# Nyström attention, routing and gated units on one core: ranks in one pass, a table loaded first, and a new order of work

## The chip, the cores and the metric

The kernel runs on one core of a Trainium2 chip. The metric is the time of one execution on the device in microseconds (us), and less is better. Three timed runs of the kernel before gave 581.68, 582.09 and 582.16 us.

## What is computed

Four batches of 576 tokens with 8 heads of 64 go through Nyström attention with 32 landmarks a head. The 2304 rows of 512 that come out are routed to one of 8 experts each, and the result passes through a gated layer of 1536 columns. The core of the reference:

```
q_lm, k_lm = means of 18 tokens each          # 32 landmarks a head
A = softmax(q k_lm'), Bm = softmax(q_lm k_lm'), C = softmax(q_lm k')
Z = Bm' / (norm1(Bm) * norminf(Bm) + 1e-6)
for _ in range(6): Z = 2 * Z - Z @ Bm @ Z
x = A @ Z @ C @ v                              # 2304 rows of 512
logits = x @ w_gate; expert_idx = argmax(logits); gate_w = max of softmax(logits)
for i in range(N):                             # rank of a token in its expert, in order
    if counts[e] < capacity: disp[e, counts[e]] = x[i]; counts[e] += 1
y = relu(disp @ w1) @ w2;  out[i] = gate_w[i] * y[expert_idx[i], pos[i]]
result = (sigmoid(out @ w_gate2) * (out @ w_val)) @ w_out
```

## The kernel before

**Tiling.** TensorE multiplies with 128 partitions of contraction. A product of good accuracy is made in three passes (`PASSES`, L22) over a number split into a high part (`hi`, rounded to the fast format) and the rest (`lo`). Attention of a batch is never multiplied out to rows: its left factor (`at`, the weights A turned and scaled with the gates) stays apart from the right one (`cv`), and the right one is multiplied into an expert's first matrix (`fold`, tile `fold_now`). So an expert's first product over a batch is `mm<-xa` or `mm<-xb`, on tiles of 128x288.

**Blocks.** A batch whose tokens sit with one expert is one block. "lead" is the block of batch 0, for the expert of its token 0; the next one is that of batch 1; the others come from a list that the kernel makes of the counts (`block_list`). After each block's expert (1024 inner columns, product tile `slot`) comes a unit: the gated layer on the same 576 rows, in twelve steps `f`, whose output collects in five accumulators `acc0` to `acc4`; the last four steps are held back and multiplied at the end, accumulator by accumulator (`unit_out`, `HELD`, `ENDS`), and each finished accumulator is copied to `o_tile` and sent off by an indirect DMA of POOL. With this input there are three expert blocks of 576 rows and three units of 768.

**What sets the order.** Each piece of work is a generator (a stream) that yields an engine and the events and buffers that it needs, and then issues instructions. `Streams.go` (L99 to L280) keeps a model of the time of each engine and always takes the stream with the smallest start in the model plus `SLACK` (0.003 us) times its urgency (`URGENCY`, L26). A large number lets others go ahead by 0.3 us per hundred. `SPARED` sets how much earlier DVE must be than ACT to get a copy that either can make. Where TensorE would have little to do, `fill_up` puts in products of no use on the tile `idle`. The order is made when the program is built and then stands; the engines run it in their own order and wait for each other by semaphores. Every operation recorded this way has line L94 in the profile.

**Streams of a batch,** in the order of the data: `load_qk` and `load_v` (SP's queue; at most eight such DMAs are open, since each uses one of eight semaphores in turn, and the DMA that comes back to a semaphore waits for the one that had it), `sums` (landmarks `ld` by DVE), `scores` (products `pa` of q with `ld`, `pb` of the landmarks; the tile `pa` is turned into `ea` by DVE), `inverse` (softmax of `pb` by ACT into `eb`, by DVE into `bb`; norms by `pn`, then `py`, `pz`), `weights` (softmax of `ea`: DVE `ma`, subtraction and sums, ACT exponential, POOL the product with `ra`), `context` (`pc`, ACT `ec`, `pct`, `pv`), `back` (the fold with the router, `pf`, `pw`, `pgt`, `pg`, whose result are the logits; then DVE makes maximum `mx`, difference `dl`, place `mn`, and `lead`, the number of the expert that SP's queue reads to load its matrices `w_raw`), `ranks`, and `gate`, `rows`, `scaled` (DVE spreads the gates as `spread`, PE makes `pgb` of it, DVE scales `at`, ACT casts the high part and DVE subtracts it for the low part of `xa`).

**Ranks before.** `ranks(b)` runs once per batch and waits for the table of the batch before. It makes a one-hot of `mn` in a scan tile of 96x48, its sum `rsum`, two products `pr` (ranks within the batch and the counts of those before), three shifted additions, the rank `r`, the mask of `cap_f`, a tile `spots` and six products `ptb` that write the list of rows by expert (`table_i`). For the lead batches a product `pe` places the lead's own row.

**Start.** Identity, masks and iotas are made on POOL and DVE; `capacity` is loaded by POOL's queue (L394) and cast on DVE (L396). ACT loads the table of its exponential when the first one comes. DVE adds the landmarks of batch 0 as the loads land.

Of the kernel before, what the change touches and what calls it, by code (L numbers as in the profile page):

```python
# [26 lines left out]
    load=60,  # L27
    sums=150,
    inverse=5,
    scores=-100,  # L30
    context=-20,
    back=10,
    weights=60,
    ranks=4,
    lead_rows=0,
    rows=5,
    lead_loads=10,
    lead_split=-20,
    fold=-20,
    lead=20,  # L40
    narrow=40,
)
STEP = 2
SUMS = ()
LOWS = "pool"
SLACK = 0.003
# [52 lines left out]
class Streams:  # L99
# [7 lines left out]
    SPARED = 1.5  # L107
# [176 lines left out]
def tile_attention_moe_glu(  # L284
# [60 lines left out]
    nc.gpsimd.memset(ones, 1.0)  # L345
    iota_c = once.tile([128, P], F32, name="iota_c")
# [13 lines left out]
    spots = once.tile([P, J, E, TC], F32R, name="spots")  # L360
# [153 lines left out]
    def urgency(stage, b):  # L514
        if b == B - 1 and stage in ("inverse", "context", "back", "ranks"):
            return 0
        return URGENCY[stage] + (STEP * b if b in range(B) else 0)

# [187 lines left out]
    def unit_out(b, idx):  # L706
# [12 lines left out]
        for c in ENDS:  # L719
            for f in range(KG - HELD, KG):  # L720
                yield "pe+", *needs(f, c)
                out_rows(b, c, f)
            run.spawn(store_out(c, idx, scatters), run.urgency)
# [67 lines left out]
    with actx:  # L791
# [7 lines left out]
        scans = []  # L799
        for i in range(3):  # L800
            t = ap.tile([P, 4 + J, E], F32, name=f"scan{i}")
            nc.gpsimd.memset(t, 0.0)
            scans.append(t)
        gates = ap.tile([P, B, J], F32, name="gates")
        counts = ap.tile([P, B + 1, E], F32, name="counts")
        nc.gpsimd.memset(counts[:, 0], 0.0)
        wrs = [ap.tile([128, G, LM], F32, name=f"wr{i}") for i in range(2)]
        for t in wrs:
# [5 lines left out]
            nc, dict(bank=7, raw=3, cv=2, qk=6, ea=2, ec=2, xs=1, w=4, ws0=1, ws1=1, ws2=1, ws3=1)  # L814
# [50 lines left out]
        def sums(b, w, g, src):  # L865
            ld = lds[b % 2]
            free = [f"{what}{b - 2}" for what in ("scores", "context", "inverse")]
            for kk in range(2):
                dv = src[:, kk].rearrange("p (c m r) -> p m c r", c=J, r=SEGP)
                dst = ld[:, w, 2 * g + kk]  # L870
                if (b, w) not in SUMS:
                    yield "dve", f"raw{b}{w}{g}{kk}", *free
                    dve.tensor_reduce(dst, dv, AX.XY, ALU.add)
                else:
                    yield "pool", f"raw{b}{w}{g}{kk}", *free
                    s3 = wk.tile([128, J, LM], F32, tag="s3", name=f"s3{w}{b}{g}{kk}", bufs=1)
                    dc = src[:, kk].rearrange("p (c m r) -> p c m r", c=J, r=SEGP)
                    pool.tensor_tensor(s3, dc[..., 0], dc[..., 1], ALU.add)
                    pool.tensor_tensor(s3, s3, dc[..., 2], ALU.add)
                    pool.tensor_tensor(s3[:, 0:3], s3[:, 0:3], s3[:, 3:6], ALU.add)  # L880
                    pool.tensor_tensor(dst, s3[:, 0], s3[:, 1], ALU.add)
                    pool.tensor_tensor(dst, dst, s3[:, 2], ALU.add)
            run.done(f"landmarks{b}{w}{g}")
# [77 lines left out]

        def scores(b):

            ld = lds[b % 2]
            for u in range(2):
# [15 lines left out]
                if u == 1 and b >= 2:  # L981
                    run.release("qk", "qk")
# [8 lines left out]
        def weights(b, u, ea):  # L991
# [6 lines left out]
            yield ("dve",)  # L998
            dve.tensor_tensor(ef, ef, ma.unsqueeze(2).broadcast_to(shape), ALU.subtract)
# [9 lines left out]
            yield ("pool",)  # L1009
            pool.tensor_tensor(ef, ef, ra.unsqueeze(2).broadcast_to(shape), ALU.mult)  # L1010
# [42 lines left out]
        def context_parts(b):  # L1053
# [15 lines left out]
            if b >= 2:  # L1069
                run.release("qk", "qk")  # L1070
# [32 lines left out]
        def back(b):  # L1103
# [64 lines left out]
            mn = wk.tile([P, J], F32, tag="mn", name=f"mn{b}")  # L1168
            yield ("dve",)
            dve.tensor_reduce(mn, eq, AX.X, ALU.min)  # L1170
            if b < LEADS:
# [3 lines left out]
                dve.tensor_scalar_add(lead[:, b, 0:1], mn[0:1, 0:1], 1000.0)  # L1175
# [4 lines left out]
            run.spawn(ranks(b, mn), urgency("ranks", b))  # L1180

        def ranks(b, mn):
            je = [P, J, E]

            def small(tag, shape, dt=F32):
                return wk.tile(shape, dt, tag=tag, name=f"{tag}{b}", bufs=1)

            yield "dve", f"table{b - 1}"
            oh = scans[0][:, 4 : 4 + J]
            dve.tensor_tensor(  # L1190
                oh, iota_m.unsqueeze(1).broadcast_to(je), mn.unsqueeze(2).broadcast_to(je), ALU.is_equal
            )

            rsum = small("rsum", [P, E])
            yield ("dve",)
            dve.tensor_reduce(rsum, oh.rearrange("p j e -> p e j"), AX.X, ALU.add)
            yield "pe", "bank"
            pr = pst([P, E], f"pr{b}")
            pe.matmul(pr, tri, rsum, start=True, stop=False)
            pe.matmul(pr, ones[0:P].broadcast_to([P, P]), counts[:, b], start=False, stop=True)  # L1200
            yield ("dve",)
            incl = small("incl", je)
            for step, dst in enumerate((scans[1][:, 4 : 4 + J], scans[2][:, 4 : 4 + J], incl)):
                src, sh = scans[step], 1 << step
# [301 lines left out]
```

## Time and profile before

| | before |
|---|---|
| timed runs, median | 582.09 us |
| the profiled execution's own time | 579.26 us |
| its span in the trace | 577.5 us |
| PE busy | 554.2 us, 96% |
| PEld (weight loads) busy | 494.4 us, 86% |
| DVE busy | 352.1 us, 61% |
| ACT busy | 249.0 us, 43% |
| POOL busy | 49.2 us, 9% |
| mean granted clock of TensorE | 0.994 |

PE is TensorE's products, PEld its weight loads, which overlap them. The span is the part of the execution that the trace shows; 1.8 us of the profiled execution lie around it. "[0.78 <-PE pa]" behind an instruction says that its engine stood idle for 0.78 us before it and that the end of `pa` on PE ended this. SPq is SP's own queue, DMAs issued there.

### The profile page before, as it was taken

To read this page: it belongs to the slowest core of one execution; us is meant where nothing else is said; L and a number is where in the kernel's file an instruction comes from. 1 tells how busy PE (TensorE), PEld (TensorE's weight loads), DVE (VectorE), ACT (ScalarE), POOL (GpSimd) and SP (SyncE) were. 2 spreads that over 40 slices of the span, in tenths; PEclk is the share of its full clock that TensorE was granted. 3 is DMA by queue.
4 is the path that set the end of the run, shared out by engine and by line. 5 is a ranking of instruction groups with operands and counts; after the bars stand their busy time and mean duration, and the time that the engine had idled before them with its cause. 6 is when DMAs were issued, how large, how long until landed. Compare 5 with 4: busy or idle time off the path is not lost. (4 is left out here: it accounts for less than half of the span.)

```text
span 577.5 us, 12424 instructions
## 1 busy us (share of the span) xinstructions
PE 554.2 (96%) x4984; PEld 494.4 (86%) x4984; DVE 352.1 (61%) x871; ACT 249.0 (43%) x563; POOL 49.2 (9%) x61
## 2 busy tenths in 40 slices
PE   8789999889999999999999999999999999999994
PEld 3347878668899999999999999999899999999983
DVE  5788798688767999999544443443373434343431
ACT  0425624245438777686333333333362333333320
POOL 2010421102510000000020000000200000000011
PEclk9899999999999999999999999999999999999998
DMA  8867826854565555562240000001250000000001
GB/s 241 232 185 262 240 83 207 248 173 155 148 262 153 182 171 191 168 197 83 70 168 1 1 1 0 2 1 50 91 164 1 1 1 1 1 1 0 1 38 49
DMA packets 30143, 60.98 MB, mean 106 GB/s; under 512 B 2848, under 2 KB 12704, under 8 KB 29696
## 3 DMA queue, kind: packets, MB, share of 16 engines
q1 hardware_dynamic: 28944, 56.58, 31.3%
q0 software_dynamic: 1136, 3.54, 1.7%
q8 instruction: 41, 0.67, 0.5%
q14 instruction: 22, 0.18, 0.1%
HBM read 46.88 MB, written 13.24 MB: 104 GB/s over the span
## 5 line engine op out<-in xcount | busy, mean ns | idle before, releaser
L94 PE MATMUL mm<-xa,ws 128*128 128x288 f32 x1344 | 187.2, 296 | 0.5 <-ACT sg L94 0.4
L94 PEld LDWEIGHTS mm<-xa,ws 128*128 128x128 f32 x1344 | 182.1, 188 | 4.6 <-issue 0.7
L94 PE MATMUL acc<-ws,slot 128*128 128x512 f32 x504 | 123.1, 391 | 1.7 <-DVE slot L94 1.7
L94 PEld LDWEIGHTS acc<-ws,slot 128*128 128x128 f32 x504 | 92.0, 188 | 19.0 <-ACT slot L94 1.9
L94 PE MATMUL mm<-xb,ws 128*128 128x288 f32 x672 | 94.2, 296 | 0.0
L94 PEld LDWEIGHTS mm<-xb,ws 128*128 128x128 f32 x672 | 91.1, 188 | 1.9
L94 PE MATMUL mm<-slot,ws 128*128 128x288 f32 x576 | 82.5, 298 | 0.0
L94 PEld LDWEIGHTS mm<-slot,ws 128*128 128x128 f32 x576 | 77.2, 188 | 2.4 <-issue 1.6
L94 ACT CAST slot<-sg 128x288 fp32r<-128x288 f32 x72 | 31.2, 433 | 65.5 <-DVE sg L94 65.4
L94 DVE TENSOR_TENSOR sg<-mm,sg 128x288 f32<-128x288 f32 x72 | 32.7, 454 | 32.7 <-PE mm L94 31.6
L94 DVE TENSOR_TENSOR slot<-sg,slot 128x288 fp32r<-128x288 f32 (+2 forms) x108 | 36.2, 355 | 22.6 <-ACT slot L94 22.6
L94 DVE TENSOR_TENSOR ws<-wo_res,ws 128x512 fp32r<-128x512 f32 x36 | 24.8, 690 | 34.7 <-ACT ws L94 34.6
L94 DVE TENSOR_TENSOR ws<-wg_res,ws 128x512 fp32r<-128x512 f32 x36 | 24.8, 690 | 27.2 <-ACT ws L94 27.1
L94 DVE TENSOR_TENSOR ws<-wv_res,ws 128x512 fp32r<-128x512 f32 x36 | 24.9, 690 | 25.9 <-ACT ws L94 25.7
L94 ACT CAST ws<-wo_res 128x512 fp32r<-128x512 f32 x36 | 22.4, 622 | 37.9 <-PE acc L94 28.3
L94 ACT CAST ws<-wg_res 128x512 fp32r<-128x512 f32 x36 | 22.3, 620 | 31.5 <-PE mm L94 27.0
L94 ACT CAST ws<-wv_res 128x512 fp32r<-128x512 f32 x36 | 22.2, 617 | 23.9 <-PE mm L94 23.5
L94 POOL TENSOR_TENSOR ws<-w_raw,ws 128x512 fp32r<-128x512 f32 x16 | 22.1, 1382 | 98.2 <-ACT ws L94 98.0
L94 ACT ACTIVATE sg<-mm 128x288 f32<-128x288 f32 x72 | 29.2, 406 | 2.0 <-PE mm L94 1.7
L94 ACT ACTIVATE slot<-mm 128x288 fp32r<-128x288 f32 x48 | 19.8, 412 | 17.8 <-PE mm L94 17.7
L94 DVE SCALAR_TENSOR_TENSOR slot<-mm,slot 128x288 fp32r<-128x288 f32 x48 | 21.5, 454 | 5.1 <-ACT slot L94 4.5
L94 PE MATMUL idle<-ones,ident 128*128 128x512 f32 (+6 forms) x38 | 21.1, 683 | 1.8 <-POOL ident masks.py:199 1.8
(202 smaller groups left out, 510.6 us busy)
## 6 DMA issues: line engine op xcount, KB each, us to landing
w_raw<-in_moe_w SPq DMA_DIRECT2D x48, 256.0 KB, 3.0
raw_g<-in_moe_w_gate SPq DMA_DIRECT2D x12, 512.0 KB, 3.6
raw_v<-in_moe_w_val SPq DMA_DIRECT2D x12, 512.0 KB, 3.8
raw_o<-in_moe_w_out SPq DMA_DIRECT2D x12, 512.0 KB, 4.2
vs<-in_v SPq DMA_DIRECT2D x4, 1152.0 KB, 10.4
out<-zeros SPq DMA_DIRECT2D x18, 256.0 KB, 4.6
slot<-in_q SPq DMA_DIRECT2D x8, 288.0 KB, 9.3
slot<-in_k SPq DMA_DIRECT2D x8, 288.0 KB, 9.3
```

The costliest lines, as they stand in the source:

```text
L94: return getattr(self.engine, op)(*args, **kwargs)
```

## The change

`URGENCY` gets other numbers throughout (load 60 to 150, scores -100 to 10, context -20 to 0, ranks 4 to 20, lead_rows 0 to 10, lead_loads 10 to 40, lead_split -20 to 100, fold -20 to 0, narrow 40 to 80), and `SPARED` falls from 1.5 to 0.6. An activation of one column right behind the memset of `ones` brings ACT's table load to the start of its queue. `capacity` is loaded on SP's queue behind `v` and the router; `v` is loaded in four DMAs of two heads. The subtraction for `lo` goes from DVE to POOL for all four batches. The ranks, spots and lists of all batches are made in one pass behind the last batch's context, with tiles of 96x192 in place of 96x48. `leads` makes what the lead blocks need of `mn`, and `block_list` adds the counts itself, with seven products in place of two. At a unit's end accumulators 0 and 1 are finished first, then the products of accumulators 4 and 2 that need steps before the last, then the others. Two places are prepared and not used here: `SUMS` stays empty, and `SUBS` and `NORMS` name the engines that had this work before.

```diff
 URGENCY = dict(
-    load=60,
+    load=150,
...
+XLO = ("pool", "pool", "pool", "pool")
...
-    SPARED = 1.5
+    SPARED = 0.6
...
+    warm = once.tile([128, 1], F32, name="warm")
+    nc.scalar.activation(warm, ones, AF.Exp)
...
-    nc.gpsimd.dma_start(cap_i, capacity.bitcast(I32).partition_broadcast(128))
     cap_f = once.tile([128, 1], F32, name="cap_f")
-    nc.vector.tensor_copy(cap_f, cap_i[:, 0:1])
...
+        held = [(c, f) for c in ENDS for f in range(KG - HELD, KG)]
+        early = [(c, f) for c, f in held if c in ENDS[-3:-1] and f < KG - 1]
+        first = [(c, f) for c, f in held if c in ENDS[:-3]]
+        for c, f in first + early + [part for part in held if part not in first + early]:
+            yield "pe+", *needs(f, c)
+            out_rows(b, c, f)
+            if f == KG - 1:
+                run.spawn(store_out(c, idx, scatters), run.urgency)
...
-            nc.sync.dma_start(vs, v[b])
+            for h in range(0, H, 2):
+                nc.sync.dma_start(vs[:, h : h + 2], v[b, :, h : h + 2])
             if b == 0:
                 nc.sync.dma_start(wrt, w_router)
+                nc.sync.dma_start(cap_i, capacity.bitcast(I32).partition_broadcast(128))
...
+        def ranks():
+            bje = [P, B, J, E]
+            yield "pool", f"context{B - 1}"
+            pool.memset(big[:, 0 : 3 * wide], 0.0)
+            yield "dve", *[f"mn{b}" for b in range(B)]
+            dve.tensor_copy(cap_f, cap_i[:, 0:1])
+            dve.tensor_tensor(oh[:, :, 4:], iota_m.unsqueeze(1).unsqueeze(1).broadcast_to(bje), mb, ALU.is_equal)
+            dve.tensor_reduce(rsum[:, B - 1 :], oh[:, :, 4:].rearrange("p b j e -> p b e j"), AX.X, ALU.add)
+            pr = pst([P, B, E], "pr")
+            for d in range(B):
+                pe.matmul(
+                    pr, tri if d == 0 else ones[0:P].broadcast_to([P, P]), rsum[:, B - 1 - d : 2 * B - 1 - d],
+                    start=(d == 0), stop=(d == B - 1),
+                )
...
+            ptb = pst([128, B * E * TC], "ptb")
             for j in range(J):
...
+        def leads():
+            yield "pe", "bank", *[f"mn{b}" for b in range(LEADS)]
+            ph = pst([NBLK, LEADS], "pe")
...
             hi, lo = (part[:, :, u] for part in x)
             act.copy(hi, at[:, :, u])
-            yield ("dve",)
-            dve.tensor_tensor(lo, at[:, :, u], hi.bitcast(F32), ALU.subtract)
+            yield (XLO[b],)
+            getattr(run, XLO[b]).tensor_tensor(lo, at[:, :, u], hi.bitcast(F32), ALU.subtract)
...
         def block_list():
-            yield "pe", "bank"
+            yield "pe", "bank", "leads"
             pk = pst([NBLK, 2], "pk")
             for i in range(2):
+                for d in range(i, B):
...
+        run.spawn(ranks(), urgency("ranks", B - 1))
+        run.spawn(leads(), urgency("ranks", 0))
```

What the new numbers make of the order is seen at three places. First DVE at the start, where batch 0's tile `pa` is turned into `ea` (`ld_156` in the kernel before, `ld_155` and `ld_156` in the changed one are the landmarks of batches 0 and 1). Before:

```order
L94 TENSOR_REDUCE ld_156<-slot_183 128x32
L94 TENSOR_REDUCE ld_156<-slot_188 128x32 x2
L94 STREAM_TRANSPOSE ea_214<-pa_215 128x288
L94 STREAM_TRANSPOSE ea_214<-pa_216 128x288
L94 STREAM_TRANSPOSE ea_225<-pa_226 128x288
L94 STREAM_TRANSPOSE ea_225<-pa_227 128x288
L94 TENSOR_REDUCE mb_249<-pb_239 128x1
L94 TENSOR_REDUCE mb_249<-pb_240 128x1
L94 TENSOR_SCALAR mb_249<-mb_249 128x2
```

After the change:

```order
L98 TENSOR_REDUCE ld_155<-slot_182 128x32 x2
L98 TENSOR_REDUCE ld_156<-slot_187 128x32
L98 STREAM_TRANSPOSE ea_212<-pa_213 128x288
L98 TENSOR_REDUCE mb_233<-pb_223 128x1
L98 STREAM_TRANSPOSE ea_212<-pa_214 128x288
L98 TENSOR_REDUCE mb_233<-pb_224 128x1
L98 STREAM_TRANSPOSE ea_235<-pa_236 128x288
L98 TENSOR_SCALAR mb_233<-mb_233 128x2
L98 STREAM_TRANSPOSE ea_235<-pa_237 128x288
```

The first sum of batch 1 (`slot_187`) has moved in ahead of the first transpose, and the three steps of `mb` now stand between the transposes.

Second, DVE behind batch 0's logits (`mx`, `dl`, `eq`, `mn`, `sgm`, `lead` and `spread` are batch 0's; `mb_570` and `ea_575` are batch 1's). Before:

```order
L94 TENSOR_REDUCE mx_559<-pg_553 96x6
L94 TENSOR_TENSOR dl_561<-pg_553,mx_559 96x48
L94 TENSOR_SCALAR eq_564<-dl_561 96x48
L94 TENSOR_TENSOR eq_564<-eq_564,iota_c 96x48
L94 TENSOR_REDUCE sgm_595<-gexp_566 96x6
L94 TENSOR_REDUCE mn_594<-eq_564 96x6
L94 TENSOR_SCALAR sgm_595<-sgm_595 96x6
L94 TENSOR_SCALAR lead<-mn_594 1x1
```

After the change:

```order
L98 TENSOR_TENSOR dl_573<-pg_554,mx_571 96x48
L98 TENSOR_REDUCE mb_570<-pb_560 128x1
L98 TENSOR_SCALAR eq_589<-dl_573 96x48
L98 TENSOR_REDUCE mb_570<-pb_561 128x1
L98 TENSOR_TENSOR eq_589<-eq_589,iota_c 96x48
L98 TENSOR_SCALAR mb_570<-mb_570 128x2
L98 TENSOR_REDUCE sgm_612<-gexp_592 96x6
L98 TENSOR_REDUCE mns<-eq_589 96x6
L98 STREAM_TRANSPOSE ea_575<-pa_576 128x288
L98 TENSOR_SCALAR sgm_612<-sgm_612 96x6
L98 TENSOR_SCALAR rb_598<-rb_598 128x2
L98 TENSOR_SCALAR lead<-mns 1x1
```

Four small steps and one transpose of batch 1 have moved in between batch 0's maximum and its expert number.

Third, PE at the end of the last unit (`mm` are the last step's value products, `slot3` is the last step's gated result). Before:

```order
L94 MATMUL acc4_2810<-ws0_68,slot2_6667 128x512 x2
L94 MATMUL mm_6740<-xa_134,ws3_71 128x288 x6
L94 MATMUL acc4_2810<-ws1_69,slot3_6738 128x512 x2
L94 MATMUL acc2_2808<-ws4_2765,slot0_6512 128x512 x3
L94 MATMUL acc2_2808<-ws5_2766,slot1_6596 128x512 x3
L94 MATMUL acc2_2808<-ws0_68,slot2_6667 128x512 x3
L94 MATMUL acc2_2808<-ws1_69,slot3_6738 128x512 x3
```

After the change:

```order
L98 MATMUL acc4_2733<-ws0_68,slot2_6590 128x512 x2
L98 MATMUL acc2_2731<-ws4_2688,slot0_6435 128x512 x3
L98 MATMUL acc2_2731<-ws5_2689,slot1_6519 128x512 x3
L98 MATMUL acc2_2731<-ws0_68,slot2_6590 128x512 x3
L98 MATMUL mm_6663<-xa_133,ws3_71 128x288 x6
L98 MATMUL acc4_2733<-ws1_69,slot3_6661 128x512 x2
L98 MATMUL acc2_2731<-ws1_69,slot3_6661 128x512 x3
```

The nine products of accumulator 2 that need no last step have moved from behind the value products `mm` to ahead of them; behind `mm` there still comes a product of `slot3` first.

## Rows read from the trace of the kernel before

**Rows 1.** Busy time by stretch: stretch and length, each engine's busy time, granted clock.

```profile
38.00:51.00 13.00, 11.66 (x271) 7.58 (x269) 11.72 (x43) 6.08 (x17) 0.00 (x0) 1.00 0.72 259
...
71.30:129.00 57.70, 52.78 (x888) 43.10 (x881) 46.90 (x143) 22.14 (x67) 10.03 (x8) 1.00 0.58 178
129.00:180.20 51.20, 50.26 (x507) 46.15 (x497) 37.98 (x116) 24.83 (x57) 13.27 (x10) 1.00 0.55 178
180.20:562.00 381.80, 381.44 (x2624) 360.26 (x2622) 209.37 (x430) 173.94 (x358) 12.05 (x12) 1.00 0.19 63
```

**Rows 2.** PE's waits from 58 to 182 us: total, times, longest.

```profile
PE mm L94 <- DMA w_raw<-in_moe_w: 1.9, 1, 1.9
PE pgb L94 <- DVE spread L94: 1.6, 3, 0.7
PE pct L94 <- ACT ec L94: 0.7, 1, 0.7
```

**Rows 3.** Timeline, batch 0's ranks and lists on PE: start, duration, instruction.

```profile
40.11 0.31 PE L94 MATMUL pr<-rsum,tri 96*96 96x8 f32 x2 [0.17 <-PE pc L94]
40.44 1.22 PE L94 MATMUL pgb<-spread,ones 96*128 96x288 f32 x4
...
48.76 0.84 PE L94 MATMUL ptb<-spots,shift 96*128 96x40 f32 x6
49.54 1.20 PE L94 MATMUL pa<-slot,ld 64*32 64x288 f32 x32
```

**Rows 4.** Timeline of the start: transposes, table load, inverse.

```profile
15.57 1.58 DVE L94 STREAM_TRANSPOSE ea<-pa 128x288 f32<-128x288 f32 x4 [0.78 <-PE pa L94]
17.36 0.17 DVE L94 TENSOR_SCALAR mb<-mb 128x2 f32<-128x2 f32 x1
...
17.61 1.28 ACT L94 ACT_TABLE_LOAD   x1 [17.61 <-DVE mb L94]
18.91 0.29 ACT L94 ACTIVATE eb<-pb,mb 128x32 f32<-128x32 f32 x1
20.55 0.49 PE L94 MATMUL pn<-bb,mask 128*128 128x128 f32 x2 [2.55 <-DVE bb L94]
```

**Rows 5.** Timeline of SP's queue: batch 1's third load of k.

```profile
15.94 0.33 SPq L841 DMA_DIRECT2D slot<-in_k  x1
```

**Rows 6.** Busy time in stretches of 2 us.

```profile
18.00:20.00 2.00, 0.00 (x0) 0.00 (x0) 0.53 (x4) 1.54 (x5) 0.00 (x0) 1.00 1.00 201
...
22.00:24.00 2.00, 2.00 (x18) 0.44 (x24) 1.70 (x7) 0.51 (x1) 0.00 (x0) 0.50 0.89 314
```

**Rows 7.** Timeline, the same 32 products `pc` in batches 0 and 1.

```profile
23.26 1.78 PE L94 MATMUL pc<-slot,ld 64*32 64x288 f32 x32
...
38.74 1.20 PE L94 MATMUL pc<-slot,ld 64*32 64x288 f32 x32
```

**Rows 8.** Timeline from batch 0's expert number to the first expert product.

```profile
39.06 0.14 DVE L94 TENSOR_SCALAR lead<-mn 1x1 int32<-1x1 f32 x1
39.36 0.46 DVE L94 TENSOR_TENSOR spread<-ident,gates 96x288 f32<-96x288 f32 x1
40.20 1.93 SPq L542 DMA_DIRECT2D w_raw<-in_moe_w  x4
50.98 1.83 PE L94 MATMUL mm<-xa,ws 128*128 128x288 f32 x12 [0.17 <-DVE ea L94]
```

**Rows 9.** Subtractions and their neighbours: DVE's timeline, and POOL's groups (min/median/max ns).

```profile
44.24 0.75 DVE L94 TENSOR_TENSOR xa<-at,xa 128x576 fp32r<-128x576 f32 x1
79.10 1.52 DVE L94 TENSOR_TENSOR spread<-ident,gates 96x288 f32<-96x288 f32 x1
L94 POOL TENSOR_TENSOR ea<-ea,ra x8: 1152/1160/1170, 29.8 to 150.8; 128x576 f32<-128x576 f32 x8
```

**Rows 10.** Timeline of PE at the last unit's end.

```profile
561.06 0.96 PE L94 MATMUL mm<-xa,ws 128*128 128x288 f32 x6
563.76 6.16 PE L94 MATMUL acc<-ws,slot 128*128 128x512 f32 x26 [1.74 <-DVE slot L94]
```

More of the change, by code (lines that the diff above doesn't have):

```diff
@@ L26 @@
 URGENCY = dict(
-    load=60,
+    load=150,
     sums=150,
     inverse=5,
-    scores=-100,
-    context=-20,
+    scores=10,
+    context=0,
     back=10,
     weights=60,
[L34 to L39, printed above, removed]
+    ranks=20,
+    lead_rows=10,
+    rows=10,
+    lead_loads=40,
+    lead_split=100,
+    fold=0,
     lead=20,
-    narrow=40,
+    narrow=80,
 )
 STEP = 2
+AHEAD = 0
 SUMS = ()
 LOWS = "pool"
+XLO = ("pool", "pool", "pool", "pool")
+SUBS = ("dve", "dve", "dve", "dve")
+NORMS = ("pool", "pool", "pool", "pool")
 SLACK = 0.003
@@ L798, in tile_attention_moe_glu @@
         wrt = ap.tile([128, KD, E], F32, name="wrt")
[L799 to L803, printed above, removed]
+        mns = ap.tile([P, B, J], F32, name="mns")
         gates = ap.tile([P, B, J], F32, name="gates")
-        counts = ap.tile([P, B + 1, E], F32, name="counts")
-        nc.gpsimd.memset(counts[:, 0], 0.0)
+        rsum = ap.tile([P, 2 * B - 1, E], F32, name="rsum")
+        nc.gpsimd.memset(rsum[:, 0 : B - 1], 0.0)
         wrs = [ap.tile([128, G, LM], F32, name=f"wr{i}") for i in range(2)]
@@ L960, in inverse, with unload @@
             run.done(f"inverse{b}")
+        def unload(b, w):
+            yield None, *[f"landmarks{b}{w}{g}" for g in range(G)]
+            run.release("qk", "qk")
         def scores(b):
@@ L1195, in ranks @@
             yield ("dve",)
-            dve.tensor_reduce(rsum, oh.rearrange("p j e -> p e j"), AX.X, ALU.add)
+            dve.tensor_reduce(rsum[:, B - 1 :], oh[:, :, 4:].rearrange("p b j e -> p b e j"), AX.X, ALU.add)
+            run.spawn(block_list(), urgency("back", B - 1))
             yield "pe", "bank"
-            pr = pst([P, E], f"pr{b}")
-            pe.matmul(pr, tri, rsum, start=True, stop=False)
-            pe.matmul(pr, ones[0:P].broadcast_to([P, P]), counts[:, b], start=False, stop=True)
+            pr = pst([P, B, E], "pr")
@@ L1206, in ranks @@
+            for step, (src, dst) in enumerate(((oh, sc[:, :, 4:]), (sc, sd[:, :, 4:]), (sd, rk))):
+                sh = 1 << step
+                dve.tensor_tensor(dst, src[:, :, 4 : 4 + J], src[:, :, 4 - sh : 4 + J - sh], ALU.add)
             yield ("dve",)
-            rk = small("rk", je)
-            dve.tensor_tensor(rk, incl, pr.unsqueeze(1).broadcast_to(je), ALU.add)
+            dve.tensor_tensor(rk, rk, pr.unsqueeze(2).broadcast_to(bje), ALU.add)
             run.release("bank")
             yield ("dve",)
-            dve.tensor_tensor(counts[:, b + 1], counts[:, b], rsum, ALU.add)
@@ L1256, in ranks @@
                 dve.scalar_tensor_tensor(done, iota_p[0:NBLK], e0, done, ALU.is_equal, ALU.add)
[L1257 to L1260 removed]
+            run.done("leads")
         def gate(b, dl, at):
@@ L1368, in lead_idx @@
         def lead_idx(b):
-            yield "dve", f"table{b}"
+            yield "dve", "table"
             c_lead = nc.vector.value_load(lead[0:1, b, 1:2], min_val=0, max_val=NCOL - TC)
             dve.tensor_copy(lead_rows[b][3], table_i[:, bass.ds(c_lead, TC)])
+            run.done(f"idx{b}")
         def finish():
-            yield None, "blocks", *[f"{what}{b}" for b in range(B) for what in ("rows", "table")]
+            yield None, "blocks", "table", *[f"idx{b}" for b in range(LEADS)], *[f"rows{b}" for b in range(B)]
             run.done("attention")
         run.spawn(finish(), 0)
+        run.spawn(ranks(), urgency("ranks", B - 1))
+        run.spawn(leads(), urgency("ranks", 0))
         run.spawn(zero_rows(), 200)
```

142 lines of the change are left out of this document (64 added, 78 removed).

## The prediction

> **What bounds the kernel now.** I read the table of busy times first: TensorE (PE) is busy for 554.2 of 577.5 us, the next engine, DVE, for 352.1. Then the same by stretch [rows 1]. From 180.20 to 562 us PE works for 381.44 of 381.80 us, so nothing but less PE work can shorten that part. From 71.30 to 129 it stands idle for 57.70 - 52.78 = 4.9 us, from 129 to 180.20 for 0.9, from 38 to 51 for 1.3. The list of PE's waits names what ended them [rows 2]: 1.9 us for one load of an expert's matrix, 1.6 us in three waits for `spread`, 0.7 us for the exponential of the context. The first 38 us and the last 14 us are chains in which engines wait for each other, and there I read the timelines. So four things can move the time: PE work taken out, the start, PE's waits before 180 us, and the end. The sum is made on the profiled execution (579.26 us, span 577.5) and the difference is put on the median, 582.09, which lies 2.8 us above it; no term depends on those 2.8.
>
> **Ranks in one pass: -2.2 us.** Per batch PE made two products `pr`, from 40.11 to the next product at 40.44, 0.33 us in four passes of 0.083, and six products `ptb`, from 48.76 to 49.54, 0.78 us [rows 3]. Four batches are 4 x 1.11 = 4.4 us, and two small `pe` of two passes each add 0.3: 4.8 us. Afterwards `pr` is four products of 32 columns, eight passes, 0.66 us. `ptb` is still six products, of 160 columns in place of 40: at least the old 0.13 each, and at most the 0.16 of a product of 288 columns (0.96 for six [rows 10]), taken 0.87. `block_list` has five products more, ten passes, 0.83 us; the one `ph` is 0.17. Together 2.5, so 4.8 - 2.5 = 2.3 and, since the new `pr` and `pk` might cost more per pass, 2.2 (bounds 1.7 and 2.4). This is work on the bounding engine in stretches that are nearly full, so it goes from the end. DVE saves some 6 us of small steps too, which is worth nothing by itself. POOL's memset of 96x960 is bounded by 960/576 of its product at 1.16 [rows 9], 1.9 us, from zero; behind it stands the subtraction of batch 2, whose product comes after 180 us: nothing. The lists are made late, at about 165 us, but what needs them first, the scatters of the first unit and the third block, comes after 180: also nothing; without that cover the third block would wait for the whole pass.
>
> **The start: -0.5 us.** Before, the chain is: transposes at 15.57, `mb` scaled at 17.36, table load 17.61 to 18.89, exponential at 18.91, and `pn` at 20.55, for which PE had waited 2.55 us [rows 4]. With the table in place early (ACT had stood idle for 17.61 us, so the load costs nothing there), 1.28 us leave this chain. But the order puts batch 1's first landmark sum in front of the first transpose. It waits for its load, and SP issues batch 1's third load of k at 15.94 [rows 5], a DMA whose semaphore was free only when that first load of batch 1 had landed. So the sum can hardly start before 15.94; at 0.75 us it ends at 16.69, and the transposes start 1.1 us later. In their favour, `mb` now stands between them and is scaled after the third, not after the fourth: 0.4 us. So 1.28 - 1.1 + 0.4 = 0.6, taken 0.5. Bounds: 0.2 lost, if the load lands later still, and 2.8 gained (a rival below). The row shows the exponential 0.02 us after the table load's end. The Trainium skill ("ScalarE: Activation LUTs", What ACT_TABLE_LOAD costs) gives 1.283 us for the load and 1.380 us more for a drain; by that 1.4 us more would leave the chain and the time would be 1.4 lower, but the row has no room for a drain behind the load, and I go by the row.
>
> **`v` in four loads, `capacity` on SP: nothing.** Four DMAs more stand in SP's queue at batch 0, 0.33 us each [rows 5], 1.3 us in all, ahead of later loads; what waits behind them is batch 1's and 2's q and k, whose sums are on no chain of PE's after 25 us. `capacity` is first needed in `ranks` at about 160 us.
>
> **From batch 0's logits to its first expert product: +0.4 us.** In DVE's order four small steps (0.17 as the scaled `mb` [rows 4]) and one transpose (1.58/4 = 0.40) of batch 1 now stand before `lead`: 1.1 us later; a reciprocal, a transpose and a product more, 0.8, stand before `spread`. Behind `lead` waits SP's register read with the loads `w_raw` at 40.20, behind `spread` PE's `pgb` [rows 3, 8]. From `lead` at 39.06 to the first product `mm<-xa` at 50.98 lie 11.9 us in which PE is idle for some 1.3. Bounds: -0.3, if PE has batch 1's inverse to do meanwhile and the old 0.17 before `mm<-xa` goes, and +1.1, all of it. I take 0.4, since the old idle time is the nearest row for how seldom PE runs dry there.
>
> **PE's waits from 71 to 180 us: -2.4 us.** The order puts the first fold for the second expert twelve products later; twelve such products take 1.83 us [rows 8], so the load that PE waited 1.9 us for is about in time. Attention of batches 2 and 3 stands some 45 products earlier against the experts' products, which gives the `pct` wait (0.7) and one of the `spread` waits (0.6) slack: 3.2 in all. Against that I set one new wait of the old kind, 0.8. Bounds: 5 gained (nearly all 5.9 idle us) and 1 lost.
>
> **The subtractions on POOL: nothing on the path.** Eight go, 0.75 us each on DVE, and become eight of 1.16, POOL's time for the same tile [rows 9]: DVE -6.0, POOL +9.3 us, each low part 0.41 later. The first ran at 44.24 and its product starts at 50.98. What they may cost DVE is a rival.
>
> **The end of a unit: 0.** At the last unit PE waits 1.74 us between the last six value products and the last step's products [rows 10], since the gated result must be made by ACT and DVE. The nine products moved ahead stand before the six value products, not behind them, where they would have filled the gap. The value products start nine x 0.237 = 2.1 us later, PE's sum is the same, and the gap stays. Bounds -0.3 and +0.8: fewer products (17 in place of 26) lie behind the gap, so the scatters follow each other closer.
>
> **Sum:** -2.2 - 0.5 + 0.4 - 2.4 + 0 = -4.7, so 582.1 - 4.7 = 577.4 us.
>
> **Rivals.** *The start gives all of it.* If batch 1's load has landed by 15.5, the 1.1 comes back, and PE's idle time before `pn` falls under 2 us. PE's granted clock fell to 0.50 of full speed (1.2 GHz) in 22 to 24 us, after it had done nothing from 18 to 20 [rows 6]; without that the 32 `pc` take 1.20 in place of 1.78 [rows 7], and as much again is saved on what lies around them: -2.8 in place of -0.5, 575.1 us. For it: the fall stands right behind the idle stretch. Against: row 5.
>
> *POOL holds up DVE.* Beside POOL's products one `spread` took 1.52 us, another without them 0.46 [rows 8, 9], 1.06 more. With eight more POOL operations of 1.16 in the same stretches 8 x 1.06 = 8.5 us more of DVE time may be held, some of it on the chain to `pgb` and `pct`. Then the waits come back elsewhere and the term of -2.4 becomes +0.5: 580.3 us. For it: DVE is busy for 46.9 of 57.7 us there [rows 1]. Against: DVE loses some 12 us of work in all. The Trainium skill says the same ("SBUF — State Buffer", Who interferes with whom): a VectorE operation with two inputs in SBUF and a GpSimd operation that reads SBUF block each other for a whole instruction; the rows agree, and the rule speaks against this part of the change.
>
> *Slower: the clock falls between 38 and 51 us.* The late `lead` and `spread` make PE wait there, and the clock falls as it did at 22. The 11.66 us of work in that stretch [rows 1] would take 1.78/1.20 as long [rows 7], 5.6 us more, and with 1.5 us of waits the sum is -4.7 + 7.1 = +2.4: 584.5 us. It decides from a loss of 4.7 + 1.2 = 5.9 on, so only if nearly the whole stretch is slow. Against: idle products still stand in the order there, about as many columns as before.
>
> *The end does what it seems meant for.* If PE in fact fills the gap at the last unit, 1.7 us go: 575.7 us.
>
> **How the numbers follow.** The forecast has 0.52, the full start 0.17, POOL's hold 0.16, the slow clock 0.10, the filled end 0.05. A change under 0.2%, 1.2 us, is about what a measurement of this kernel can't tell from none, so 580.9 to 583.3 counts as the same. Faster: 0.48 of the forecast, the full start, the filled end and 0.10 of POOL's hold, 0.80. Slower: 0.09. The same: 0.11. The range 573.0 to 582.5 leaves out the slow clock and the outer ends of the others, some 0.17.
>
> **What would show it.** After: four groups `pr` and 24 `ptb` gone, `ptb` x6 under 1 us; the transposes at about 16.7 and `pn` at about 20.0; `lead` about 0.6 later than 39.06; no wait of 1.9 us for `w_raw` before 180, and idle PE time from 71 to 180 of about 3.5 us; PE's wait for `slot` at the last unit still about 1.7; PE busy for some 552 us. I am wrong if `pn` moves by more than 1.5 us, if the granted clock is under 0.9 in any stretch after 30 us, or if PE's waits for DVE before 180 us grow over the old 1.6.

## The result and the profile after

The changed kernel takes 566.84 us (median of four runs, 565.13 to 568.24) against 581.88 of four runs of the kernel before: a ratio of 0.9752, 95% interval 0.9708 to 0.9796, 15.0 us between the medians. In a second set of runs, beside other runs of before with a median of 579.06, it took 568.38 (567.23 to 571.56), ratio 0.9815 (0.9777 to 0.9852), 10.7 us. The forecast was 577.4 with a range of 573.0 to 582.5: the direction was right, the size a third of what came in the first set, under half of what came in the second, and both times the result lies outside the range.

Its profiled execution took 565.13 us, span 563.3. The busy times by engine:

```profile
span 563.3 us, 12343 instructions
PE 545.8 (97%) x4966; PEld 490.1 (87%) x4966; DVE 345.9 (61%) x826; ACT 249.6 (44%) x564; POOL 59.3 (11%) x66
```

How much of the 14.2 us between the spans is won by 180.2 us is read from PE's work that is left from there to the end (busy time and count are the second pair of numbers; first the kernel before, then the changed one):

```profile
180.20:590.00 409.80, 387.62 (x2650) 365.06 (x2648) 212.15 (x436) 175.33 (x361) 14.91 (x15) 0.99 0.18 61
180.20:590.00 409.80, 373.06 (x2548) 350.94 (x2546) 197.21 (x406) 161.80 (x335) 15.08 (x15) 0.99 0.16 54
```

The changed kernel has 102 products, 14.6 us, less to do from there. So in these two executions all of it is won in the first 180 us, and nothing of it in the dense part behind. The stretches of [rows 1], now of the changed kernel:

```profile
0.00:38.00 38.00, 32.95 (x470) 16.45 (x470) 31.85 (x109) 9.90 (x35) 4.36 (x20) 1.00 0.77 249
38.00:51.00 13.00, 12.59 (x314) 10.07 (x318) 11.34 (x31) 9.18 (x26) 2.81 (x2) 1.00 0.84 279
71.30:129.00 57.70, 57.67 (x1042) 47.70 (x1040) 47.81 (x143) 28.14 (x84) 16.21 (x13) 1.00 0.63 200
129.00:180.20 51.20, 49.24 (x375) 46.55 (x374) 39.92 (x93) 30.01 (x59) 10.69 (x9) 1.00 0.59 195
```

PE's idle time falls from 6.45 to 5.05 us up to 38, from 1.34 to 0.41 up to 51, from 4.92 to 0.03 between 71.3 and 129, and rises from 0.94 to 1.96 behind: 6.2 us in all. PE's work of single kinds, over the whole execution (idle products, `pr`, `ptb`, `pk`, `pc`, `pa` in this order, before and then after):

```profile
0.00:590.00 590.00, 21.08 (x38) 0.99 0.33 103
0.00:590.00 590.00, 1.84 (x16) 0.99 0.33 103
0.00:590.00 590.00, 3.25 (x24) 0.99 0.33 103
0.00:590.00 590.00, 0.28 (x4) 0.99 0.33 103
0.00:590.00 590.00, 5.70 (x128) 0.99 0.33 103
0.00:590.00 590.00, 6.62 (x128) 0.99 0.33 103
...
0.00:590.00 590.00, 18.75 (x38) 0.99 0.32 103
0.00:590.00 590.00, 0.87 (x8) 0.99 0.32 103
0.00:590.00 590.00, 0.90 (x6) 0.99 0.32 103
0.00:590.00 590.00, 0.60 (x14) 0.99 0.32 103
0.00:590.00 590.00, 4.80 (x128) 0.99 0.32 103
0.00:590.00 590.00, 5.80 (x128) 0.99 0.32 103
```

Ranks and lists take 2.37 in place of 5.37 us, 3.0 less; idle products 2.3 less; and the same 256 products `pc` and `pa` take 1.7 us less. With the 6.2 us of idle time that is 13.2 of the 14.6; the rest lies in small groups. The idle products and the products `pc` and `pa` are as many as before. A part of what they lost is the clock: the traced execution of before has a granted clock of 0.78, 0.50 and 0.87 in the three stretches of 2 us from 20 to 26 us, which by estimate is 2 x (0.22 + 0.50 + 0.13) = 1.7 us of work; the changed kernel's has 1.00 there.

The start, in the timeline of the changed kernel (for [rows 4, 7]):

```profile
6.37 4.41 DVE L98 TENSOR_REDUCE ld<-slot 128x32 f32<-128x576 f32 x6 [1.31 <-DMA slot<-in_q]
10.95 0.75 DVE L98 TENSOR_REDUCE ld<-slot 128x32 f32<-128x576 f32 x1 [0.17 <-DMA slot<-in_q]
12.28 0.48 DVE L98 STREAM_TRANSPOSE ea<-pa 128x288 f32<-128x288 f32 x1 [0.57 <-PE pb L98]
13.84 0.29 ACT L98 ACTIVATE eb<-pb,mb 128x32 f32<-128x32 f32 x1 [11.61 <-DVE mb L98]
15.63 0.49 PE L98 MATMUL pn<-bb,mask 128*128 128x128 f32 x2 [0.74 <-DVE bb L98]
17.36 1.20 PE L98 MATMUL pc<-slot,ld 64*32 64x288 f32 x32
31.62 0.60 PE L98 MATMUL pg<-pick,lt 128*96 128x16 f32 x6
```

`pn` has moved from 20.55 to 15.63. Batch 0's logits `pg` stood at 37.25 before:

```profile
37.25 0.60 PE L94 MATMUL pg<-pick,lt 128*96 128x16 f32 x6
```

They come 5.6 us earlier; this is the start's share of what is won in these two executions. In a second traced execution of the changed kernel (after_again) `pn` stands at 16.40 and `pg` at 32.39, 0.8 us later: so much is chance. Batch 0's and batch 1's sums were ready far earlier than the forecast had them: the sum of batch 1 that I placed at 15.94 ran at 10.95.

### The profile page after: what moved, and what is told of

It is laid out like the page before. It is cut to its first block, busy times and chain, and to the rows that moved or that the text cites. A ratio compares the mean times of both kernels' runs of the same rounds, so it can differ in the third digit from the quotient of the medians.

```text
span 563.3 us, 12343 instructions
## 1 busy us (share of the span) xinstructions
PE 545.8 (97%) x4966; PEld 490.1 (87%) x4966; DVE 345.9 (61%) x826; ACT 249.6 (44%) x564; POOL 59.3 (11%) x66
## 5 line engine op out<-in xcount | busy, mean ns | idle before, releaser
L98 PE MATMUL mm<-slot,ws 128*128 128x288 f32 x576 | 81.1, 298 | 0.0
L98 ACT ACTIVATE slot<-mm 128x288 fp32r<-128x288 f32 x48 | 19.7, 410 | 15.7 <-PE mm L98 15.1
L98 POOL TENSOR_TENSOR ws<-w_raw,ws 128x512 fp32r<-128x512 f32 x16 | 20.6, 1301 | 32.7 <-ACT ws L98 24.3
L752 POOL DMA_INDIRECT out<-o_tile,idx_two x5 | 4.8, 966 | 149.5 <-DVE o_tile L98 146.8
```

What stands on the lines that cost most here:

```text
L98: return getattr(self.engine, op)(*args, **kwargs)
L752: scatter = nc.gpsimd.indirect_dma_start(out[:, :], bass.IndirectOffsetOnAxis(ap=idx[0:n, c : c + 1], axis=0), o[0:n], None, bounds_check= ...
```

## The experiments

An experiment's ratio is always against runs of the kernel before on the same chip. The kernel before scatters itself, 576.5 to 584.8 us beside these experiments, so that four runs of a kernel tell differences of some 0.5 to 0.9%.

**Capacity's load.** The kernel, the queue and the place were changed one at a time:

```diff
+    nc.gpsimd.dma_start(cap_i, ...)        # cap_pool: in the changed kernel, at the old place
+    nc.sync.dma_start(cap_i, ...)          # cap_sp_first: in the changed kernel, ahead of q and k
...
                 nc.sync.dma_start(wrt, w_router)
+                nc.sync.dma_start(cap_i, ...)  # before_cap: in the kernel before, from POOL to here
```

> The changed kernel with the load of capacity back on POOL's queue, at its old place. In the trace of the changed kernel the third landmark sum of batch 0 starts at 6.37 us, before at 8.11, and the inverse's first product pn at 15.63 in place of 20.55. Theory A (capacity's load, issued at 2.3 us, stood in the way of the loads of q and k): the third sum goes back to about 8, pn to 18.5 to 19.5 (the early table load stays), and the time to 570 to 571 us. Theory B (the other order of work and the four loads of v made the start early): third sum at 6.4, pn at 15.6, time 567.

> The changed kernel with the load of capacity on SP's queue but ahead of all loads of q and k. Theory A1 (what hurts is that it runs while batch 0's landmarks are loaded, on whatever queue): the third sum at 8 and pn at 18.5 or later, about 570 us, as with capacity on POOL. Theory A2 (what hurts is POOL's queue): as the changed kernel but for the 0.4 us that one more issue takes, pn at about 16, 567 us.

> The kernel before with one part of the change alone: capacity is loaded on SP's queue behind v and the router, and its cast stands in the first ranks. Theory A: pn at 17 to 17.5 in place of 20.55 (the late table load stays), time 582 - 3.5 = 578.5 us. Theory B: nothing, 582 us.

Measured: 571.49 us with capacity on POOL (ratio 0.9842, 0.9780 to 0.9904), 568.76 with it first on SP (0.9809, 0.9758 to 0.9859), and 579.69 in the kernel before (1.0003, 0.9969 to 1.0037). The stretch from 5 to 8 us (last two columns: share of the DMA engines, GB/s) of before, the changed kernel, cap_pool and cap_sp_first:

```profile
5.00:8.00 3.00, 3.00 (x5) 1.20 (x4) 0.09 (x1) 0.00 (x0) 0.00 (x0) 1.00 0.79 152
5.00:8.00 3.00, 3.00 (x8) 1.21 (x7) 1.67 (x4) 0.00 (x0) 0.00 (x0) 1.00 0.99 343
5.00:8.00 3.00, 3.00 (x6) 1.25 (x5) 0.87 (x2) 0.00 (x0) 0.00 (x0) 1.00 0.81 196
5.00:8.00 3.00, 3.00 (x7) 1.10 (x6) 2.53 (x4) 0.00 (x0) 0.00 (x0) 1.00 1.01 361
```

With 1 KB for capacity on POOL's queue the loads move at about half the rate, while the DMA engines are shown busy for 0.79 and 0.81 of the time. It is so in every trace of this study: 152 to 206 GB/s in the five with capacity on POOL's queue, 343 to 383 in the fifteen with it on SP's. The loads come late by it. In the kernel before the third sum of batch 0 waited 3.02 us:

```profile
8.11 0.76 DVE L94 TENSOR_REDUCE ld<-slot 128x32 f32<-128x576 f32 x1 [3.02 <-DMA slot<-in_q]
```

The last sum of batch 0 ends at 12.5 to 14.8 us in the five traces and at 10.2 to 11.5 in the fifteen. In cap_pool the third sum ran at 6.10, not at 8 as theory A had it; a later one waited 2.62 us, to 9.48.

`pn` stands at 18.25 in cap_pool, 16.11 in cap_sp_first, and 17.49 in before_cap (20.55 before). The 20.55 is in part chance: ranks_only below, with the loads and the table load of the kernel before, has `pn` at 18.98. So it is POOL's queue that costs more than the moment: theory A2 is nearer than A1. The test is not clean, since cap_sp_first changes the queue and the moment at once, and on SP's queue the load is not free either: from 2 to 5 us the loads moved 207 GB/s there, against 288 in the changed kernel. In time, cap_pool against the changed kernel is not clear of the scatter, and before_cap gained nothing in the median though its start is 3 us earlier. That was the puzzle.

**The early table load, the loads of v, and the start as a whole.** The edits:

```diff
-    nc.scalar.activation(warm, ones, AF.Exp)   # no_warm: in the changed kernel
...
-            for h in range(0, H, 2):               # v_one: in the changed kernel
-                nc.sync.dma_start(vs[:, h : h + 2], v[b, :, h : h + 2])
+            nc.sync.dma_start(vs, v[b])
```

In the kernel before, the opposite edits make before_warm (early table), before_cap_warm (capacity on SP and early table), before_cap_v4 (capacity on SP and v in four) and start_only (all three).

> The changed kernel without the early activation. The table load of 1.28 us stands in the chain between mb and the first exponential again. If the chain of the start bounds the time, pn goes from 15.63 to 16.9 and the time to 568.1 us; if PE also falls back to its lower clock behind the longer wait, as in the kernel before, 569 to 570. If the start is hidden by then, 566.8.

> The changed kernel with v in one load per batch. If the four loads matter (a quarter of v lets q and k of later batches through earlier): 568 to 569 and sums of batch 1 later than 24.0; if not, 566.8.

> The kernel before with the whole start of the change and nothing else: capacity on SP's queue behind v, v in four loads, the early table load. pn at about 15.7 in place of 20.55. If 4.9 us at the start carry through: 577, a ratio of 0.9915. If, as with the load of capacity alone, they are given back behind 38 us: a ratio of 0.997 or more, with the lower clock or longer waits after 30 us.

> The kernel before with the early table load alone. Theory K (the 1.28 us matter twice: they shorten the chain, and with the shorter wait before pn PE keeps its full clock at 20 to 25 us and later): pn about 19.3, no stretch at 0.5 of full speed before 60 us, the 32 pc of batch 0 in 1.20 us, and a ratio of 0.994 or less. Theory V (the four loads of v are what the start as a whole had and capacity alone had not): a ratio of 0.998, from the 1.28 us alone.

> The kernel before with capacity on SP's queue and the early table load, v still in one load. Theory K: as with the whole start (ratio 0.989), full clock throughout. Theory V: nearer to capacity alone, 0.996 or more.

> The kernel before with capacity on SP's queue and v in four loads, the table load late. Theory K: as with capacity alone (ratio 1.000), with the clock at half around 20 and 40 us. Theory V: 0.993 or less.

| | us | ratio | interval |
|---|---|---|---|
| capacity on SP alone | 579.69 | 1.0003 | 0.9969 to 1.0037 |
| early table alone | 578.74 | 0.9981 | 0.9957 to 1.0004 |
| capacity and early table | 575.97 | 0.9923 | 0.9897 to 0.9949 |
| capacity and v in four | 576.40 | 0.9934 | 0.9910 to 0.9958 |
| all three (start_only) | 574.42 | 0.9889 | 0.9814 to 0.9965 |
| changed kernel without early table | 570.52 | 0.9829 | 0.9780 to 0.9878 |
| changed kernel, v in one load | 567.53 | 0.9766 | 0.9688 to 0.9843 |

Neither without the early table nor with v in one load is the time of the changed kernel clear of its own scatter. In start_only `pn` came at 17.28, not at the expected 15.7. Its trace shows why:

```profile
1.85 11.00 PE L94 MATMUL idle<-ones,ident 128*128 128x512 f32 x18 [1.85 <-POOL ident masks.py:199]
6.06 4.50 DVE L94 TENSOR_REDUCE ld<-slot 128x32 f32<-128x576 f32 x6 [0.94 <-DMA slot<-in_q]
12.78 1.20 PE L94 MATMUL pa<-slot,ld 64*32 64x288 f32 x32
```

All eight sums of batch 0 (the last six are shown) have ended at 10.56, but `pa` starts at 12.78, right behind 18 idle products that stand first in PE's order. In all fifteen traces with capacity on SP's queue `pa` starts as these products end, at 11.3 to 12.8 us (11.47 in the changed kernel). So once the loads are fast, not they but the products of no use set when batch 0's scores begin.

What became of the 3 us of before_cap is seen in its clock. Two stretches of before_cap, and the same two of before_cap_v4 (third number from the end: granted clock):

```profile
20.00:22.00 2.00, 2.00 (x41) 0.87 (x26) 2.00 (x7) 0.06 (x1) 0.00 (x0) 0.50 1.02 395
40.00:42.00 2.00, 2.00 (x7) 1.46 (x8) 1.72 (x10) 2.00 (x7) 0.00 (x0) 0.50 0.83 260
...
20.00:22.00 2.00, 2.00 (x50) 0.88 (x34) 1.87 (x7) 0.61 (x3) 0.00 (x0) 1.00 0.85 323
40.00:42.00 2.00, 2.00 (x15) 1.13 (x19) 1.72 (x10) 2.00 (x7) 0.00 (x0) 1.00 0.90 226
```

In before_cap PE ran at 0.50 (1.2 GHz) at 20 to 22 and again at 40 to 42 us, and behind 100 us it waited 2.2 us for `w_raw`; by 180.2 us it was only 0.3 us ahead of the kernel before (387.31 against 387.62 us of PE work left). Its ten runs lie far apart, 576.76 to 584.34, with mean granted clocks of 0.984 to 0.998. Theory K, that the early table is what keeps the clock, does not hold as put: before_cap_v4 has the late table and the same wait of 2.6 us before `pn`, and kept the full clock. Theory V does not hold either: capacity with the early table gains as much (0.9923) as capacity with v in four. The early table alone brings no more than its 1.28 us in time, though `pn` came at 16.98 in its trace, 3.6 us earlier than before. So in the medians either of the two makes capacity's load count.

The runs' mean granted clocks show what lies under this. The kernel before took 576.5 to 578.7 us in its eight runs, over all chips, with a mean of 0.995 or more (median 577.9), and up to 584.8 in the others. At 0.995 or more, capacity alone has a median of 576.9 (two of its ten runs), the early table alone 576.9 (four of twelve), both 575.8 (six of seven), capacity and v in four 576.2 (five of eight), and start_only 574.4 (all four). So at a like clock capacity is worth 0.9 us, the table 1.0 and both 2.1: these parts do add, as far as so few runs tell. What differs is how many runs keep the clock. In before_cap_v4's trace both clock falls and PE's wait for `w_raw` are gone. In before_cap_warm's, of its slowest run (581.23 us, the one under 0.995), the clock is full up to 60 us and then 0.50 from 108 to 112, behind two waits for `w_raw` of 3.5 us in all.

Why the clock falls in one execution and not in another, these runs do not show. The same wait of 2.5 to 2.6 us before `pn` has a fall behind it in two kernels' traces (before, before_cap) and none in two others (ranks_only below, before_cap_v4); in before_urg, below, a wait of 2.18 us has one.

**Ranks, urgencies, subtractions.** The edits are ranks_only (the kernel before with the one pass and what belongs to it), all_but_ranks (the changed kernel with ranks per batch), and three of a line:

```diff
+URGENCY = dict(load=60, ...), SPARED = 1.5      # old_urgency: in the changed kernel
...
+URGENCY = dict(load=150, ...), SPARED = 0.6     # before_urg: in the kernel before
...
-XLO = ("pool", "pool", "pool", "pool")          # lo_dve: in the changed kernel
+XLO = ("dve", "dve", "dve", "dve")
```

> The changed kernel with the urgencies and SPARED of the kernel before; the loads, the early table, the ranks in one pass and POOL's subtractions stay as changed. Theory U (the new order of the batches' work against the experts' products is worth most, since it is what fills PE's waits between 38 and 180 us): 573 to 576 us, PE idle 5 us or more between 70 and 180 us again. Theory S (the early start carries over to the end by itself): 567 to 569.

> The kernel before with the new urgencies and SPARED alone: capacity on POOL's queue, late table load, ranks per batch, subtractions on DVE. Theory U: 573 to 576 us. Theory S: 580 to 582, no change.

> The kernel before with the ranks of all batches in one pass (and the leads, the block list and the release of the q and k tiles that belong to it) alone: old urgencies, capacity on POOL's queue, late table load, v in one load, subtractions on DVE, old unit end. Theory P (the pass is worth the PE work that it saves): 582 - 2.2 = 579.8 at the level of the runs of before that go with it, a ratio of 0.996. Theory D (the ranks per batch also held up DVE, which is over 80% busy from 38 to 129 us and which PE waits for there): a ratio of 0.988 or less, 575, with PE's idle time from 71 to 180 us under 4 us.

> The changed kernel with the ranks per batch as before. Theory P: 566.8 + 2.2 = 569. Theory D: 573 or more, as much above the changed kernel as its DVE is fuller, with waits of PE between 38 and 180 us.

> The changed kernel with the eight subtractions of the low parts on DVE again. If DVE's time between 38 and 150 us bounds the batches' attention, the 6 us that return to DVE make PE wait: 569 to 571. If POOL's reads held DVE up as feared (8 x 1.06 us), they are gone with it and the time is the same or lower, 565 to 567.

Measured: old_urgency 569.05 us (0.9813, 0.9751 to 0.9875), before_urg 586.67 (1.0122, 1.0059 to 1.0185), ranks_only 573.12 (0.9878, 0.9802 to 0.9954), all_but_ranks 588.96 (1.0175, 1.0084 to 1.0265), lo_dve 567.62 (0.9788, 0.9726 to 0.9850).

Theory U falls: with the old urgencies the changed kernel keeps nearly everything, and the new ones alone make the kernel before slower. The product of ranks_only and start_only, 0.9878 x 0.9889 = 0.977, is as much as the whole change; with intervals of 0.8% on either side this does not show that the other parts are worth nothing. With the ranks per batch and the new urgencies the last list is made late. In before_urg:

```profile
176.07 0.20 DVE L94 TENSOR_SCALAR table_i<-ptb 128x40 int32<-128x40 f32 x1 [0.53 <-PE ptb L94]
176.37 0.33 SPq L509 DMA_DIRECT2D raw_g<-in_moe_w_gate  x1
180.08 0.65 ACT L94 ACTIVATE raw_g<-raw_g 128x512 f32<-128x512 f32 x1 [7.54 <-DMA raw_g<-in_moe_w_gate]
185.23 7.26 PE L94 MATMUL mm<-xa,ws 128*128 128x288 f32 x36 [8.80 <-ACT ws L94]
```

The list comes at 176.07 (166.31 before, 149.01 in the changed kernel). A load of the unit's weights, `raw_g`, is issued at 176.37, after SP's queue waited 19.1 us for `pos` and 0.9 for `prow`, steps of the block list; ACT waits 7.54 us for this load and PE 8.80 for the weights made of it, and the granted clock is 0.50 from 178 to 184. In all_but_ranks PE waits 9.61 at the same place. That the late list holds up the weights is my reading of these rows; it was not tried apart. If it is right, the new urgencies need the one pass.

In ranks_only 381.16 us of PE work are left at 180.2 us, 6.5 less than before. The ratio is the one that theory D gave, but D's mark, idle time under 4 us from 71 to 180, did not come: the trace shows 0.43 + 4.56 = 5.0. So D is not shown. Of the 6.5, ranks and lists on PE are 3.0 (2.33 against 5.37 us) and idle time up to 180.2 is 0.9. But batch 0's logits, too, stand 2.3 us earlier (35.0 against 37.25) and the clock never falls up to 180 us, which in the trace of before took some 1.7 us (the estimate above). The loads are issued as before, so this part need not be the pass's own. At a mean clock of 0.995 or more ranks_only has a median of 572.9 us, 5.0 less than before and not 7: some of its ratio is before's clock. The other 2 us over the PE work saved stay open.

Of POOL's subtractions, lo_dve shows no cost and no gain in time. In the changed kernel the tiles `spots` vary (min, median and max in ns):

```profile
L98 DVE TENSOR_TENSOR spots<-rk,place_m x4: 394/874/1475, 144.3 to 147.6; 96x240 fp32r<-96x240 f32 x4
```

The slow ones stand beside POOL's subtractions of expert weights (`ws`), which are on POOL before and after; in lo_dve `spots` take 397 to 1491 ns too. What the moved subtractions held up is one step `rk`, 1.52 us beside one of them and 0.35 with them on DVE. PE waits 1.2 us for `spots` in the changed kernel and 0.2 in lo_dve.

**The end of a unit.** The changed kernel again, the order of before, and two orders that put products behind the last value products:

```diff
-            yield "pe+", *needs(f, c)
+            yield "pe+", *needs(f, c), *([f"unit_{b}{KG - 1}1"] if (c, f) in early else [])   # fill_end, fill_two
...
+        early = [(c, f) for c, f in held if c == ENDS[-3] and f < KG - 1 or c == ENDS[-2] and f == KG - HELD]   # fill_two
```

> The changed kernel as it is, beside the two others of this call: 566 to 568 us, PE's wait for the gated result at the last unit 1.7 us.

> The changed kernel with the order of products at a unit's end as before. From the 36 last value products but one group on, the trace shows 26.0 us to the end before and 26.6 in the changed kernel, since its last scatters follow each other closer; so 0.6 us less than the changed kernel if that is the order's doing, nothing if it is chance.

> The changed kernel with one more condition at a unit's end: the products of accumulators 4 and 2 that are taken early wait until the last step's value products are issued, so that they stand behind these and fill PE's wait for the gated result (1.7 us at the last unit). If that wait is all there is, it goes and the time is 565.1; if the value products wait for something themselves, the time is the same, 566.8.

> The changed kernel with nine products (accumulator 4's six that need no last step and accumulator 2's first three) behind the last value products, in PE's wait of 1.7 us, and accumulator 4 finished right behind them, so that the scatters stay apart: the wait is gone and the end comes 1.7 us + 0.6 us earlier than in the changed kernel, counted from the last 36 value products; 564.5 us.

Measured: after_again 568.38 us (567.23 to 571.56), old_end 567.56 (565.83 to 569.96), fill_two 565.70 (563.43 to 567.16) on one chip, ratios 0.9815, 0.9799 and 0.9758; fill_end, on another chip, 566.49 (0.9774). The end on PE, of the changed kernel and then of fill_two:

```profile
550.94 4.12 PE L98 MATMUL acc<-ws,slot 128*128 128x512 f32 x17 [1.74 <-DVE slot L98]
...
549.11 7.50 PE L98 MATMUL acc<-ws,slot 128*128 128x512 f32 x32
```

Before the 17 products the old wait of 1.74 us stands as in [rows 10]; in fill_two 32 products follow without one. From the start of the 36 value products ahead of this to the end of the span: before 577.5 - 551.52 = 26.0 us, changed kernel 26.6 and 26.5, old_end 565.9 - 539.88 = 26.0, fill_end 25.0, fill_two 564.1 - 540.12 = 24.0. So in these traces the new order costs 0.5 to 0.6 us, filling the wait gives 1.5 to 1.7, and scatters that stay apart 1.0 more. In time, old_end is not clear of the changed kernel; fill_two has the lowest median of this study, and no run of it was above the fastest of the changed kernel on the same chip.

## Why the prediction was wrong

**The start** is the step that failed: -0.5 us in the sum, against `pg` 5.6 us earlier and a ratio of 0.9889 for the start alone. I took from [rows 5] when batch 1's first load must have landed, 15.94, and kept that for the changed kernel; it ran at 10.95. `pn` moved by 4.9 us, over the 1.5 that I had named as a sign of being wrong. The fault lies in the part that I costed at nothing: of capacity's load I asked who waits for it, not what it does to the loads beside it. What came in its place is a load rate of 343 in place of 152 GB/s from 5 to 8 us, and batch 0's last sum at 10.8 in place of 14.8. The trace of before had it in view, in the sum that waited 3.02 us, to 8.11. I did not ask either what PE does before `pa`: its idle products ended at 12.62 before, and in the changed kernel, where they end at 11.54, they bound the start. Of the 0.9889 not all is the start's own: at a like clock start_only is 3.5 us faster than before, not 6.4. The 1.28 us of the table load left the chain as said: the exponential starts 0.10 us after the last step of `mb` ends. The rival "the start gives all of it" had its signs come true: the load in time, PE idle for 0.74 us before `pn`, the full clock, and `pc` in 1.20 us. Its -2.8 was half of the 5.6, since it left the loads of batch 0 as late as the forecast did.

**Ranks in one pass**: the PE work was right in kind, as was its going from the end, but its size lies beyond the bounds of 1.7 and 2.4: 2.2 forecast, 3.0 measured. `ptb` took 0.90 for 0.87; the old `pr` took 1.84 us, not 4 x 0.33, and the five products more of `block_list` 0.32, not 0.83. Alone the pass brought a ratio of 0.9878, some 7 us, 5.0 at a like clock; what it has beyond the 3.0 is not explained.

**From logits to the first expert product**: +0.4 had the wrong sign. `lead` came 34.09 - 31.62 = 2.5 us behind `pg` in place of 1.8, as the order showed, but the first `mm<-xa` at 44.75 came 13.1 us behind `pg`, not 13.7:

```profile
34.09 0.14 DVE L98 TENSOR_SCALAR lead<-mns 1x1 int32<-1x1 f32 x1
```

**Waits from 71 to 180 us**: -2.4 forecast, 5.86 - 1.99 = 3.9 in the traces, and 5.86 - 3.00 = 2.9 with after_again's. The wait for `w_raw` is gone and new ones (`ptb`, `pk`) are inside the pass. All waits of PE of 0.4 us and more in the whole execution:

```profile
PE idle L98 <- POOL ident masks.py:199: 1.9, 1, 1.9
PE acc L98 <- DVE slot L98: 1.7, 1, 1.7
PE pz L98 <- DVE rz L98: 1.6, 2, 0.9
PE ptb L98 <- DVE spots L98: 1.2, 1, 1.2
PE pn L98 <- DVE bb L98: 0.7, 1, 0.7
PE pct L98 <- ACT ec L98: 0.6, 1, 0.6
PE pk L98 <- DVE rsum L98: 0.4, 1, 0.4
```

I put this term down to the new order; old_urgency has 1.44 + 1.80 = 3.2 us idle in the same two stretches, so with the old order 2.6 are kept, against 2.9 and 3.9 with the new one: the other parts of the change bring most of it.

**The subtractions on POOL**: nothing on the path, as forecast; each took 1.41 to 1.75 us, not 1.16. The rival of POOL holding DVE was real in one place (`rk`) and not to be seen in the time. **The end**: 0 with +0.8 as bound, measured +0.5 to 0.6; the gap stayed, as the order said. **The slow clock** at 38 to 51 us did not come in the changed kernel, though before_cap's 0.50 at 40 to 42 shows that it can. It came elsewhere: after_again has 0.50 at 108 to 110 us. And the level, 582.1, lay some 4 us above before's runs at a mean clock of 0.995 or more (577.9); the sum had no term for that.

## What to carry to other kernels

Of a small load that is moved, ask what it does to the transfers that it ran beside, not only who waits for it: 1 KB on POOL's queue among the first loads halved their rate for three microseconds. A start that is made shorter ends at the next thing that binds; here that was 18 products of no use, put in to fill PE's time. Read the granted clock of each run beside its time: capacity's load and the early table seemed not to add, and at a like clock they do. Numbers of a planner belong to the work that they order: the new ones cost 7 us with the old ranks, and with the new no cost is seen.

## What the runs showed of the hardware

Capacity's load, 128 rows on POOL's queue, took 7.3 us to land in the kernel before, 2.9 on SP's queue ahead of everything, and 6.9 on SP's queue behind v and the router in the changed kernel. From 5 to 8 us the DMA engines were shown 79% busy at 152 GB/s in the kernel before, against 99% at 343 in the changed one. TensorE's granted clock fell to 0.50 (1.2 GHz) behind an idle stretch of 2.6 us before `pn` in two kernels' traces (before, before_cap) and stayed at 1.00 behind the same stretch in two others (ranks_only, before_cap_v4); in before_cap_warm it was 0.50 from 108 to 112 us, behind waits of 3.5 us. Over the runs of one program the time goes with the mean granted clock: 576.5 to 578.7 us at 0.995 or more, up to 584.8 below. The table load took 1.28 us with nothing else behind it: in the changed kernel `warm` ran 0.02 us after it. The Trainium skill ("ScalarE: Activation LUTs", What ACT_TABLE_LOAD costs) gives a drain of 1.38 us more for every switch to a different set; neither trace has it behind this first load, and the measurement decides.
